# A spectral filter gated with a state-space scan: one addition moved from VectorE into an accumulating DMA, skip rows and table steps re-ordered

## The chip, the cores and the metric

The kernel runs on one core of one Trainium2 chip. The core has TensorE (PE, matrix products into PSUM), VectorE (DVE), ScalarE (ACT), GpSimd (POOL), SyncE (SP, which issues most of the DMAs) and 16 DMA engines. The metric is device time in microseconds, the median of several executions.

## The reference

Two branches read the same `x` (2048 positions by 1024 channels, bf16) and are mixed by a gate per position:

```python
g = sigmoid((x * gate_w).sum(-1, keepdims=True))
# branch A: a filter in the two-dimensional spectrum
X = rfft2(x, axes=(-2, -1)) * (w_r + 1j * w_i)
a = irfft2(X, s=(S, D), axes=(-2, -1)).astype(bfloat16)
# branch B: a diagonal complex state-space model, 1024 states
Lam = Lambda_re + 1j * Lambda_im;  dt = exp(log_dt)
Lam_bar = exp(dt * Lam)
B_bar = ((Lam_bar - 1.0) / Lam)[:, None] * (B_re + 1j * B_im)
Bu = einsum("bld,pd->blp", x, B_bar)
for t in range(L): h = Lam_bar[None, :] * h + Bu[:, t, :]
b = 2.0 * einsum("blp,dp->bld", hseq, C_re + 1j * C_im).real + x * Dskip
return g * a + (1 - g) * b
```

## The kernel before, in words

**Branch A (FFT).** Both transforms are products with constant matrices. `fstage` adds and subtracts the input rows and multiplies by `FW_sb` (first stage). The main loop `fft_main` then runs over 16 groups of row frequencies. For group g, `fd(g)` does the column transform into PSUM (`ps_d`) and ACT copies it to `X1`; `bf_w(g)` does the row transform (`ps_xe`, `ps_xo`), copies it to `X` and multiplies by the weights `W` on VectorE (`Y`, L525 to L528); `bi(g)` transforms the rows back (`ps_q`). The order is fd(g+2), bf_w(g+1), bi(g). A second loop over 8 pairs (`idm`, `pm`, `fi`) does the inverse column transform and writes branch A to a scratch in DRAM, `ya_scratch`. These PSUM tiles share a pool of three buffers.

**Branch B (scan).** Time is cut into NCH = 4 chunks c of TC = 512 positions, and the 1024 states into 4 groups q of 256: 16 tiles (c, q). The complex recurrence is turned by an angle that grows with time, so that what is left is a real scan with a real factor. For each tile:

- `ssm_pe` (L388) multiplies `xT` by `BT`: 32 matmuls of 128x512 in 4 blocks of 8, one PSUM tile `psu` each (two buffers); ACT evicts and scales each block into the tile `u` (L390, two buffers).
- `ssm_dve` turns `u` forward (two products L399 and L401, one addition L403, into `cu`), scans four times (L408, into `su`), keeps the last column as the carry (L417 to L421) and turns back: two products L433 and L435 with the table reversed in time, and an addition L437 into `h`. As written, L435 puts the second product into `u` itself, and L437 adds `cu` and `u`. Where `h` lies (`h_tile`): chunks 0 and 3 in a pool of four buffers, chunk 1 in free parts of `big`, chunk 2 in parts of `xT`. `cu` and `su` have two buffers each.

The sines and cosines of the angle are in `tab`; `tables(q)` makes them when chunk 0 comes to tile q. For q < 2 VectorE computes the angle, for q of 2 and 3 ACT does (L360); VectorE takes the fraction of a turn in three steps over both halves at once (`frac`, L288 to L290, 1024 fp32 elements per partition), ACT applies Sin twice (L366, L367), VectorE negates one (L368).

**Output.** For each block tb of 128 positions, `half(tb, dh)` (L782) does 16 matmuls of `h` with `CT[dh]` for each half dh of the channels, into `psy` (three buffers). After the second half VectorE computes `o` = `psy` * (1-g) + `xf` (L789), and SP writes `o` out. `xf` is made ahead of that: SP loads rows of `x` (`xc`) and of branch A (`gac`); `prep_d` multiplies `xc` by `Dskip` on VectorE (L760); `prep_a` scales both on ACT (L764, L766) and GpSimd issues a DMA that adds `gac` into `xf` (L767). `prep_a(tb)` also issues the loads of block tb+2.

**What sets the order.** The kernel is written as two generators, the FFT (`fft_main`) and the scan (`ssm_all`), which are stepped in turn by estimated clocks `fft.t` and `ssm.t`: a line of constants near L725 says how far the scan may be for each state of the FFT, another (L728) up to where it is run before the output starts, and later L805 and L812 interleave the scan with the output blocks (`c_all`). In `ssm_all` the VectorE part of a tile runs one tile behind its matmuls; every step of `ssm_dve` ends in a `yield`. SP and GpSimd keep the written order throughout, ACT from the output part on; the order of the others is made by a scheduler that starts from this order and its own estimates. Every engine then works its list strictly in that order. `pre` in `c_all` says after which half block each `prep_d` and `prep_a` is written.

Of the kernel before, what the change touches and what calls it, by code (L numbers as in the profile page):

```python
# [10 lines left out]
ACT = mybir.ActivationFunctionType  # L11
ALU = mybir.AluOpType
FP32 = mybir.dt.float32
BF16 = mybir.dt.bfloat16
I32 = mybir.dt.int32
# [7 lines left out]
P = 128  # L23
TC = 512
NCH = S // TC
MAGIC = 12582912.0
# [110 lines left out]
def kernel(  # L137
# [17 lines left out]
    nc = tc.nc  # L155
# [130 lines left out]
    def frac(xx, n, nm, pool=sp, tag=None):  # L286
        kk = pool.tile([P, n], FP32, name=nm + "_k", **({"tag": tag} if tag else {}))
        nc.vector.tensor_scalar(out=kk, in0=xx, scalar1=MAGIC, scalar2=-MAGIC, op0=ALU.add, op1=ALU.add)  # L288
        nc.vector.tensor_sub(out=xx, in0=xx, in1=kk)
        nc.vector.tensor_scalar(out=kk.bitcast(I32), in0=xx.bitcast(I32), scalar1=0x7FFFFFFF, scalar2=None,  # L290
                                op0=ALU.bitwise_and)
        return xx, kk
# [57 lines left out]

    def tables(q):
        xa = rp.tile([P, 2 * TC], FP32, name="xa", tag="cu")
        for jj in range(2):
            jb = 2 * q + jj
            xj = xa[:, TC * jj:TC * (jj + 1)]
            if q < 2:
                nc.vector.tensor_scalar(out=xj, in0=tau_f, scalar1=thp[:, jb:jb + 1], scalar2=beta[:, jb:jb + 1],
                                        op0=ALU.mult, op1=ALU.add)
            else:
                nc.scalar.activation(out=xj, in_=tau_f, func=ACT.Identity, scale=thp[:, jb:jb + 1],  # L360
                                     bias=beta[:, jb:jb + 1])
        rr, ra = frac(xa, 2 * TC, "xa", rp, "su")
        tq = tab[:, 2 * q:2 * q + 2]
        rr = rr.rearrange("p (a t) -> p a t", a=2)
        ra = ra.rearrange("p (a t) -> p a t", a=2)
        nc.scalar.activation(out=tq[:, :, 0, :], in_=ra, func=ACT.Sin, scale=-TWO_PI_LO, bias=chpi)  # L366
        nc.scalar.activation(out=tq[:, :, 1, :], in_=rr, func=ACT.Sin, scale=-TWO_PI_LO)  # L367
        nc.vector.tensor_scalar_mul(out=tq[:, :, 2, :], in0=tq[:, :, 1, :], scalar1=-1.0)  # L368


    hs = {}
# [22 lines left out]
    def ssm_dve(c, q, u):  # L394
        tq = tab[:, 2 * q:2 * q + 2]
        full = [P, 2, 2, TC]
        cu = rp.tile(full, BF16, name="cu", tag="cu")
        su = rp.tile(full, BF16, name="su", tag="su")
        nc.vector.tensor_mul(out=cu, in0=u, in1=tq[:, :, 0:1, :].to_broadcast(full))  # L399
        yield  # L400
        nc.vector.tensor_mul(out=su, in0=u[:, :, ::-1, :], in1=tq[:, :, 1:3, :])  # L401
        yield
        nc.vector.tensor_add(out=cu, in0=cu, in1=su)  # L403
        yield
        for jj in range(2):
            jb = 2 * q + jj
            for ri in range(2):
                nc.vector.tensor_tensor_scan(out=su[:, jj, ri, :], data0=r_sb[:, jb:jb + 1].to_broadcast([P, TC]),  # L408
                                             data1=cu[:, jj, ri, :],
                                             initial=(0.0 if c == 0 else carry[q][:, jj, ri:ri + 1]),  # L410
                                             op0=ALU.mult, op1=ALU.add)
                if not (jj and ri):
                    yield
        if c + 1 < NCH:
            ge = su[:, :, :, TC - 1]
            k1 = sm.tile([P, 2, 2], FP32, name="k1")
            nc.vector.tensor_mul(out=k1, in0=ge, in1=cTC[:, 2 * q:2 * q + 2].unsqueeze(2).to_broadcast([P, 2, 2]))  # L417
            k2 = sm.tile([P, 2, 2], FP32, name="k2")
            nc.vector.tensor_mul(out=k2, in0=ge[:, :, ::-1], in1=sg[:, 2 * q:2 * q + 2, :])
            cy = sm.tile([P, 2, 2], FP32, name=f"carry{q}")  # L420
            nc.vector.tensor_add(out=cy, in0=k1, in1=k2)  # L421
            carry[q] = cy
        yield
        h = h_tile(c, q)
        hs[c, q] = h
        if False:
            nc.vector.tensor_mul(out=h, in0=su, in1=tq[:, :, 0:1, ::-1].to_broadcast(full))
            yield
            nc.vector.tensor_mul(out=cu, in0=su[:, :, ::-1, :], in1=tq[:, :, 1:3, ::-1])
            nc.gpsimd.dma_start(out=h, in_=cu, accum_op=ALU.add)  # L430
            yield
            return
        nc.vector.tensor_mul(out=cu, in0=su, in1=tq[:, :, 0:1, ::-1].to_broadcast(full))  # L433
        yield
        nc.vector.tensor_mul(out=u, in0=su[:, :, ::-1, :], in1=tq[:, :, 1:3, ::-1])  # L435
        yield
        nc.vector.tensor_add(out=h, in0=cu, in1=u)  # L437
        yield
# [250 lines left out]
    def ssm_all():  # L689
        prev = iter(())  # L690
        for c in range(NCH):
            for q in range(4):
                if c == 0:
                    tables(q)
                u = up.tile([P, 2, 2, TC], BF16, name="u", tag="u")
                for i, _ in enumerate(ssm_pe(c, q, u)):
                    yield 0.5
                    for _ in range((0,4,3,3)[i]):
                        next(prev, None)
                        yield 0.52  # L700
                prev = ssm_dve(c, q, u)
        for _ in prev:
            yield 0.72
# [18 lines left out]
    ssm = Gen(ssm_all())  # L722
    fft = Gen(fft_main())
    while not fft.done:
        if ssm.t < (18.5 * (fft.t - 3.5) / (54.4 - 3.5) if fft.t < 54.4 else 18.5 + (44 - 18.5) * (fft.t - 54.4) / 35.0):  # L725
            ssm.step()
        else:
            fft.step()  # L728
    while ssm.t < 44:
        ssm.step()  # L730
    fctx.close()

    with ExitStack() as bctx:
# [59 lines left out]
        def c_all():  # L793
            order = [(0, 0), (1, 0), (2, 0), (0, 1), (1, 1), (2, 1)] + [(tb, dh) for tb in range(3, 16) for dh in range(2)]
            pre = {(0, 0): [(prep_d, 0), (prep_d, 1)], (1, 0): [(prep_a, 0)], (2, 0): [(prep_a, 1)],
                   (0, 1): [(prep_d, 2)], (1, 1): [(prep_a, 2)], (2, 1): [(prep_d, 3)], (3, 0): [(prep_a, 3), (prep_d, 4)],
                   (3, 1): [(prep_a, 4)]}
            for n in range(5, 16):
                pre[n - 1, 0] = [(prep_d, n)]
                pre[n - 1, 1] = [(prep_a, n)]  # L800
            for tb, dh in order:
                half(tb, dh)
                for f, n in pre.get((tb, dh), ()):
                    f(n)
                yield 3.6  # L805

        while ssm.t < 48:
            ssm.step()
        cg = Gen(c_all())
        t0 = ssm.t  # L810
        while not cg.done:
            if not ssm.done and ssm.t - t0 <= cg.t * 1.05:  # L812
                ssm.step()
            else:
                cg.step()
# [30 lines left out]
```

## Time and profile before

| | |
|---|---|
| median of 3 runs | 351.5 us (351.18 to 352.78) |
| the profiled execution's own time | 353.56 us |
| its span, first to last instruction | 351.8 us |
| granted TensorE clock | 0.99 |
| PE busy | 325.6 us, 93% of the span |
| DVE busy | 297.6 us, 85% |
| ACT busy | 188.0 us, 53% |
| POOL busy | 41.9 us, 12% |
| L437, last addition of the back rotation, 16 times | 1.22 us each |
| `xf` DMA with addition, 512 KB, 16 times | 4.0 us from issue to landing |

"Busy" is the time in which an engine has an instruction running. Matmuls are pipelined, so that the time of one (379 ns for 128x512) is longer than the distance between two starts (216 ns): the distance is what counts. The profile also answers what an engine waited for, which chain of work ended last, and what ran when; line numbers are those of the kernel before.

### The profile page before, as it was taken

Reading aid. Unit: us, or ns where it says so; the run is one execution under the profiler, and the core shown is the slowest. Engines: PE = TensorE matmul, PEld = TensorE weight load, DVE = VectorE, ACT = ScalarE, POOL = GpSimd, SP = SyncE. Lnnn points to the kernel's source line nnn. Section 1 sums busy time; section 2 is a strip of 40 time slices with the busy share of each in tenths; the row PEclk is TensorE's granted clock in tenths of the full one; section 3 lists DMA queues with packets and bytes.
Section 4 is the critical chain, followed back from the end, with each engine's and each line's share of the span. In section 5 each row is a group of like instructions: output and inputs, shape, how many; then the busy total and the mean of one; then the engine's idle time right before and its main releaser. Section 6 shows DMA issues by size and latency. Waiting matters only on the chain.

```text
span 351.8 us, 4890 instructions
## 1 busy us (share of the span) xinstructions
PE 325.6 (93%) x1804; PEld 173.6 (49%) x1804; DVE 297.6 (85%) x419; ACT 188.0 (53%) x255; POOL 41.9 (12%) x89
## 2 busy tenths in 40 slices
PE   3788999889979999999999999999989998999995
PEld 1565565556545656564444444444434443444442
DVE  4998848986999969898999999989898898988431
ACT  1987969759948887587344314432413404322330
POOL 5330412112210000000011000000000000000110
PEclk9999999989989999999999999999999999999999
DMA  7979999969997022113897053422414223444963
GB/s 263 352 104 224 215 238 198 185 152 194 196 227 134 33 89 89 61 60 121 229 223 204 3 179 67 143 89 60 136 36 129 91 60 104 108 134 136 265 197 106
DMA packets 68168, 51.30 MB, mean 146 GB/s; under 512 B 52656, under 2 KB 55728, under 8 KB 68144
## 3 DMA queue, kind: packets, MB, share of 16 engines
q1 hardware_dynamic: 64144, 38.75, 43.6%
q0 software_dynamic: 3648, 12.07, 13.6%
q8 instruction: 14, 0.23, 0.3%
q10 hardware_dynamic: 352, 0.17, 0.2%
q14 instruction: 10, 0.08, 0.1%
HBM read 21.61 MB, written 8.39 MB: 85 GB/s over the span
## 4 chain that ended last, share of the span: by engine, by line
PE 63%; DVE 18%; DMA 7%; ACT 5%; issue 3%; SPq 1%; POOL 0%; DVEq 0%; ACTq 0%; POOLq 0%
PE psy L782 27%; PE psu L388 22%; DVE su L408 6%; DMA xt<-in_A_x_dram 3%; PE ps_id L557 3%; PE ps_d L488 2%; DMA xc<-in_A_x_dram 2%; DMA MM<-c_MM 1%; DVE cu L403 1%; DMA xT<-in_A_x_dram 1%; DVE cu L433 1%; DVE t L526 1%; PE ps_q L546 1%; PE ps_y L576 1%; PE ps_q L547 1%
## 5 line engine op out<-in xcount | busy, mean ns | idle before, releaser
L388 PE MATMUL psu<-xT,BT 128*128 128x512 bf16 x512 | 120.3, 379 | 4.5 <-ACT u L390 3.1
L388 PEld LDWEIGHTS <-BT 128*128 128x128 bf16 x512 | 49.7, 98 | 60.1 <-issue 5.9
L408 DVE TENSOR_TENSOR_SCAN su<-r_sb,carry,cu 128x512 bf16<-128x512 f32 x48 | 57.7, 1264 | 0.4
L390 ACT ACTIVATE u<-psu,rho 128x512 bf16<-128x512 f32 x32 | 22.1, 691 | 64.5 <-PE psu L388 46.7
L782 PEld LDWEIGHTS <-h 128*128 128x128 bf16 x256 | 25.1, 98 | 30.2
L767 POOL DMA_DIRECT2D xf<-gac x16 | 14.0, 875 | 215.4 <-ACT xf L766 201.5
L390 ACT ACTIVATE u<-psu,nrho 128x512 bf16<-128x512 f32 x32 | 22.1, 691 | 29.3 <-PE psu L388 29.3
L764 ACT ACTIVATE gac<-gac,gf 128x1024 bf16<-128x1024 bf16 x16 | 18.3, 1141 | 27.8 <-DMA gac<-ya_scratch 27.8
L782 PE MATMUL psy<-big,h 128*128 128x512 bf16 x128 | 28.9, 379 | 0.0
L782 PE MATMUL psy<-CT,h 128*128 128x512 bf16 x128 | 28.9, 379 | 0.0
L789 DVE SCALAR_TENSOR_TENSOR o<-psy,om_f,xf 128x1024 bf16<-128x1024 f32 (+1 forms) x17 | 20.6, 1214 | 7.0 <-PE psy L782 7.0
L760 DVE TENSOR_TENSOR xc<-xc,dsk_bc 128x1024 bf16<-128x1024 bf16 x16 | 11.0, 686 | 17.1 <-DMA xc<-in_A_x_dram 17.1
L399 DVE TENSOR_TENSOR cu<-u,tab 128x2048 bf16<-128x2048 bf16 x16 | 19.5, 1219 | 5.0 <-ACT u L390 4.8
L550 ACT CAST big<-ps_q 128x1024 bf16<-128x1024 f32 x16 | 16.4, 1026 | 11.2 <-PE ps_q L549 11.0
L546 PE MATMUL ps_q<-MM,Y 128*128 128x256 bf16 x64 | 16.3, 287 | 4.7 <-DVE Y L527 4.5
L782 PEld LDWEIGHTS <-big 128*128 128x128 bf16 x128 | 12.5, 98 | 15.1
L782 PEld LDWEIGHTS <-xT 128*128 128x128 bf16 x128 | 12.5, 98 | 15.1
L403 DVE TENSOR_TENSOR cu<-cu,su 128x2048 bf16<-128x2048 bf16 x16 | 19.6, 1226 | 0.3
L433 DVE TENSOR_TENSOR cu<-su,tab 128x2048 bf16<-128x2048 bf16 x16 | 19.5, 1219 | 0.1
L488 PE MATMUL ps_d<-G_sb,big 128*128 128x256 bf16 (+3 forms) x128 | 19.6, 294 | 0.0
L401 DVE TENSOR_TENSOR su<-u,tab 128x2048 bf16<-128x2048 bf16 x16 | 19.5, 1218 | 0.0
L435 DVE TENSOR_TENSOR u<-su,tab 128x2048 bf16<-128x2048 bf16 x16 | 19.5, 1217 | 0.0
(168 smaller groups left out, 559.6 us busy)
## 6 DMA issues: line engine op xcount, KB each, us to landing
xf<-gac POOLq DMA_DIRECT2D x16, 512.0 KB, 4.0
ya_scratch<-ya SPq DMA_DIRECT2D x16, 256.0 KB, 2.0
xc<-in_A_x_dram SPq DMA_DIRECT2D x16, 256.0 KB, 2.9
gac<-ya_scratch SPq DMA_DIRECT2D x16, 256.0 KB, 3.1
out_dram<-o SPq DMA_DIRECT2D x15, 256.0 KB, 2.0
MM<-c_MM SPq DMA_DIRECT2D x16, 192.0 KB, 4.3
xt<-in_A_x_dram SPq DMA_DIRECT2D x4, 512.0 KB, 4.3
CT<-in_A_x_dram SPq DMA_DIRECT2D x4, 512.0 KB, 7.8
```

The lines of the kernel that those rows point to most:

```text
L388: nc.tensor.matmul(psu, lhsT=BT[:, jb, ri, dblk, :], rhs=xT[:, dblk, TC * c:TC * (c + 1)], start=(dblk == 0), stop=(dblk == 7))
L390: nc.scalar.activation(out=u[:, jj, ri, :], in_=psu, func=ACT.Copy, scale=(nrho if ri else rho)[:, jb:jb + 1])
L399: nc.vector.tensor_mul(out=cu, in0=u, in1=tq[:, :, 0:1, :].to_broadcast(full))
L401: nc.vector.tensor_mul(out=su, in0=u[:, :, ::-1, :], in1=tq[:, :, 1:3, :])
L403: nc.vector.tensor_add(out=cu, in0=cu, in1=su)
L408: nc.vector.tensor_tensor_scan(out=su[:, jj, ri, :], data0=r_sb[:, jb:jb + 1].to_broadcast([P, TC]), data1=cu[:, jj, ri, :], initial=(0.0 ...
L433: nc.vector.tensor_mul(out=cu, in0=su, in1=tq[:, :, 0:1, ::-1].to_broadcast(full))
L435: nc.vector.tensor_mul(out=u, in0=su[:, :, ::-1, :], in1=tq[:, :, 1:3, ::-1])
L488: nc.tensor.matmul(ps[:, lo:lo + w], lhsT=FX[:, q, 8 * g:8 * g + 8, :], rhs=G_sb[:, o:o + w], start=start, stop=stop, skip_group_check=True)
L546: nc.tensor.matmul(dst, lhsT=Yr[:, e:e + 255:2], rhs=ri_, start=True, stop=False, **kw)
L782: nc.tensor.matmul(psy[:, ds], lhsT=hs[c, jb // 2][:, jb % 2, ri, P * tq:P * (tq + 1)], rhs=CT[dh][:, jb, ri, :], start=(i == 0), stop=(i ...
L789: nc.vector.scalar_tensor_tensor(out=o[:, ds], in0=psy[:, ds], scalar=om_f[:, tb:tb + 1], in1=xfs[tb][:, ds], op0=ALU.mult, op1=ALU.add)
```

## The change

- `ssm_dve`: for chunks 2 and 3, except tile (3, 3), the first back product goes straight into `h`, the second into `cu`, and the addition is a DMA issued by GpSimd that adds `cu` into `h`. `u` is then no longer written by the second product. The other nine tiles are as before.
- `tables`: each half (512 elements) is handled by itself with steps of its own, which the scan's generator issues one at a time.
- the pacing constants: 18.5 becomes 17, 44 becomes 42, 48 becomes 47, 1.05 becomes 1.08.
- `pre`: `prep_d(n)` is written behind the second half of block n-2 instead of the first half of block n-1, and the pair is issued from one list, `prep_a` first.

```diff
     def tables(q):
         xa = rp.tile([P, 2 * TC], FP32, name="xa", tag="cu")
+        kk = rp.tile([P, 2 * TC], FP32, name="xa_k", tag="su")
+        tq = tab[:, 2 * q:2 * q + 2]
         for jj in range(2):
             jb = 2 * q + jj
-            xj = xa[:, TC * jj:TC * (jj + 1)]
+            xj, kj = xa[:, TC * jj:TC * (jj + 1)], kk[:, TC * jj:TC * (jj + 1)]
             if q < 2:
                 nc.vector.tensor_scalar(out=xj, in0=tau_f, scalar1=thp[:, jb:jb + 1], scalar2=beta[:, jb:jb + 1],
                                         op0=ALU.mult, op1=ALU.add)
+                yield
             else:
                 nc.scalar.activation(out=xj, in_=tau_f, func=ACT.Identity, scale=thp[:, jb:jb + 1],
                                      bias=beta[:, jb:jb + 1])
-        rr, ra = frac(xa, 2 * TC, "xa", rp, "su")
-        tq = tab[:, 2 * q:2 * q + 2]
-        rr = rr.rearrange("p (a t) -> p a t", a=2)
-        ra = ra.rearrange("p (a t) -> p a t", a=2)
-        nc.scalar.activation(out=tq[:, :, 0, :], in_=ra, func=ACT.Sin, scale=-TWO_PI_LO, bias=chpi)
-        nc.scalar.activation(out=tq[:, :, 1, :], in_=rr, func=ACT.Sin, scale=-TWO_PI_LO)
+            nc.vector.tensor_scalar(out=kj, in0=xj, scalar1=MAGIC, scalar2=-MAGIC, op0=ALU.add, op1=ALU.add)
+            yield
+            nc.vector.tensor_sub(out=xj, in0=xj, in1=kj)
+            nc.vector.tensor_scalar(out=kj.bitcast(I32), in0=xj.bitcast(I32), scalar1=0x7FFFFFFF, scalar2=None,
+                                    op0=ALU.bitwise_and)
+            yield
+            nc.scalar.activation(out=tq[:, jj, 0, :], in_=kj, func=ACT.Sin, scale=-TWO_PI_LO, bias=chpi)
+            nc.scalar.activation(out=tq[:, jj, 1, :], in_=xj, func=ACT.Sin, scale=-TWO_PI_LO)
         nc.vector.tensor_scalar_mul(out=tq[:, :, 2, :], in0=tq[:, :, 1, :], scalar1=-1.0)
+        yield
...
-        if False:
+        if (c>=2 and (c,q)!=(3,3)):
             nc.vector.tensor_mul(out=h, in0=su, in1=tq[:, :, 0:1, ::-1].to_broadcast(full))
             yield
             nc.vector.tensor_mul(out=cu, in0=su[:, :, ::-1, :], in1=tq[:, :, 1:3, ::-1])
             nc.gpsimd.dma_start(out=h, in_=cu, accum_op=ALU.add)
             yield
             return
...
                 if c == 0:
-                    tables(q)
+                    for _ in tables(q):
+                        yield 0.0
...
-        if ssm.t < (18.5 * (fft.t - 3.5) / (54.4 - 3.5) if fft.t < 54.4 else 18.5 + (44 - 18.5) * (fft.t - 54.4) / 35.0):
+        if ssm.t < (17 * (fft.t - 3.5) / (54.4 - 3.5) if fft.t < 54.4 else 17 + (42 - 17) * (fft.t - 54.4) / 35.0):
...
-    while ssm.t < 44:
+    while ssm.t < 42:
...
-                   (0, 1): [(prep_d, 2)], (1, 1): [(prep_a, 2)], (2, 1): [(prep_d, 3)], (3, 0): [(prep_a, 3), (prep_d, 4)],
-                   (3, 1): [(prep_a, 4)]}
-            for n in range(5, 16):
-                pre[n - 1, 0] = [(prep_d, n)]
-                pre[n - 1, 1] = [(prep_a, n)]
+                   (0, 1): [(prep_d, 2)], (1, 1): [(prep_a, 2), (prep_d, 3)], (2, 1): [(prep_a, 3), (prep_d, 4)]}
+            for n in range(4, 16):
+                pre.setdefault((n - 1, 1), []).append((prep_a, n))
+                if n < 15:
+                    pre.setdefault((n - 1, 1), []).append((prep_d, n + 1))
...
-        while ssm.t < 48:
+        while ssm.t < 47:
...
-            if not ssm.done and ssm.t - t0 <= cg.t * 1.05:
+            if not ssm.done and ssm.t - t0 <= cg.t * 1.08:
```

## Prediction

> **What bounds it now.** I read the page's busy shares first, then its slices, then the waits of each engine in the last part, then the chain there and the order of time around each hole of TensorE.
>
> ```profile
> PE 325.6 (93%) x1804; PEld 173.6 (49%) x1804; DVE 297.6 (85%) x419; ACT 188.0 (53%) x255; POOL 41.9 (12%) x89
> ...
> PE   3788999889979999999999999999989998999995
> ...
> PEclk9999999989989999999999999999999999999999
> ```
>
> TensorE is the bound: sixteen 128x512 matmuls take 3.45 us in the chain, 0.216 each, so the 512 of L388 and the 512 of L782 are 221 us and the FFT's about 90. That is 311 of a span of 351.8; only the other 41 can be won. Some 15 lie before 30 us (loading) and 4 behind the last matmul, both untouched. What the edits can reach are holes of TensorE: those of the spectral loop (30 to 112 us, some 15 us of loss) and those of the last part (164 to 348 us). The waits of TensorE and of ScalarE, from 160 us on:
>
> ```profile
> PE psu L388 <- ACT u L390: 3.1, 3, 1.4
> ...
> ACT u L390 <- DVE xT L437: 11.0, 2, 6.4
> ACT u L390 <- DVE h L437: 6.8, 1, 6.8
> ```
>
> So in the last part TensorE loses 3.1 us, three times: `psu` is not evicted because `u` is not free, and `u` is not free because VectorE still reads it in the last addition (L437) of two tiles before. VectorE's round there, as the chain between 255 and 300 us gives it:
>
> ```profile
> 261.22 1.29 DVE o L789
> ...
> 262.95 2.72 DMA xc<-in_A_x_dram
> ...
> 265.69 0.69 DVE xc L760
> 266.39 1.15 DVE cu L403
> ...
> 267.56 4.82 DVE su L408 x4
> ...
> 272.40 1.22 DVE cu L433
> 273.63 1.15 DVE u L435
> ```
>
> A tile starts at 262.4 and the next at 277.1: VectorE needs 14.7 to 15.6 us for a tile of chunks 2 and 3, with 0.9 to 1.6 us of waiting for `xc`; TensorE needs 13.8 for its share (32 matmuls of each kind). The holes of the loop, in order of time, VectorE's row and then TensorE's, twice:
>
> ```profile
> 63.52 3.45 DVE L408 TENSOR_TENSOR_SCAN su<-r_sb,cu 128x512 bf16<-128x512 f32 x3
> 71.64 0.28 PE L546 MATMUL ps_q<-MM,Y 128*128 128x256 bf16 x1 [2.29 <-DVE Y L527]
> 94.24 3.45 DVE L408 TENSOR_TENSOR_SCAN su<-r_sb,cu 128x512 bf16<-128x512 f32 x3
> 102.37 0.28 PE L546 MATMUL ps_q<-MM,Y 128*128 128x256 bf16 x1 [2.26 <-DVE Y L527]
> ```
>
> Three scans, a table step and a product stand in a row on VectorE, the frequency rows' `Y` waits behind them, and TensorE for `Y`. After each hole the 256-wide matmuls start every 0.21 us instead of 0.11 for some 3.6 us: each costs about 3.8 us, not 2.3.
>
> **What the Trainium skill says.** "TensorE: Matmul & The Clock Gate", Part 1, What's actually happening: an idle TensorE falls to half its clock and needs about 3.4 us of work to get it back. The trace agrees (0.21 against 0.11, 3.6 us), though waits of about 2.3 us were enough here, while one of 1.6 us at 43 us was not. "DMA: Bandwidth & Descriptors", Rules for kernel authors: an accumulating DMA reads its destination and writes it later, so readers of `h` must wait for its landing. "SBUF — State Buffer", Who interferes with whom: a product of two tensors has no mode that takes GpSimd's write port, so VectorE's products should not starve the descriptors. Of the 16 `xf` DMAs, issued amid such work, the issue took 0.86 to 0.95 us.
>
> **The change, part by part.**
>
> *The addition.* Seven tiles (all of chunks 2 and 3 but the last) lose L437: 7 x 1.14 us (start to start; 1.22 alone) = 8.0 us off VectorE. The first product now goes into `h`, the second into `cu`, so nothing after L401 touches `u`: it comes free about 10 us sooner. With that the three TensorE waits go: 0.95 + 0.75 + 1.39 = **-3.1 us**. VectorE's round falls to 13.0 plus about 1 of `xc`, level with TensorE's 13.8, and the lead of the evictions (5 to 8 us in the trace) absorbs the rest. The other 5 us of the 8.0 are worth nothing: TensorE hides them. For them to matter the last tile's `h` (done at 321.9, wanted by the thirteenth matmul of block 12 at 322.5) would have to be late; in the new order it has some 5 us.
>
> Added are seven DMAs of 512 KB on GpSimd's queue. No row shows this one; nearest is
>
> ```profile
> xf<-gac POOLq DMA_DIRECT2D x16, 512.0 KB, 4.0
> ```
>
> The skill's fit ("DMA: Bandwidth & Descriptors", Anatomy of one DMA: 2.0 us plus bytes over 436 KB per us) gives an estimate of 3.2; I take 4 to 5, and 8 as upper end (twice `xf`, since the source is twice as large and chunk 2's destination lies in four pieces per partition). Issue: 0.9 us, at most four times that. Who waits: `cu` is wanted again two tiles on, about 13 us after the product, and block 8 or 12 of L782 later still. Up to 12 us it costs nothing; beyond that VectorE stops. The queue is in order: the new order has xf 0 to 3, tile (2,0), xf 4, (2,1), (2,2), xf 5, (2,3), then one xf and one tile by turns. So xf 5 now waits for the product of (2,2): about 241 against 238.4, landing by 247 where its reader stood at 261. Nothing on the path.
>
> *Skip rows.* In the order of VectorE and ACT `xc` and `gac` still follow the output of three blocks before; each pair of ACT copies stands one eviction later in most tiles. Row 3's product moves ahead of tile (1,3): perhaps 1 us of VectorE's wait, away from the path. Zero; from -0.3 to +0.5.
>
> *Table steps.* Per table two halves instead of one piece: three fp32 steps of 0.68, 1.216 and 0.69 become pairs of about 0.37, 0.63 and 0.37 (half the elements plus some 0.05 each): +0.15 us, four tables +0.6 on VectorE. The Sins, 1.17 and 1.07 at 1024, become two each of about 0.65: +0.35, four tables +1.4 on ACT. Counts: VectorE +12 - 7, ACT +8.
>
> *The order that results.* The pacing constants (17 for 18.5, 42 for 44, 47 for 48) move 5 L388 matmuls (1.1 us) behind the sixteenth frequency group and 8 (1.7 us) from the inverse stage to the last part: they are only put off, TensorE has the same total. What counts is holes. I walked the new order from group 5 with the durations above (a full product 1.13 and a scan 1.14 start to start, `Y` of a group 1.2 for its two products and 0.67 for its sums, each ACT copy 0.7 or 1.0). First tile: `Y` of 6 ends at 64.25; scan 65.4; `Y` of 7 with a scan in it 68.4; scan 69.55; table 2's subtraction 70.15. Its Sin now stands on ACT ahead of X1(9): 70.85, X1(9) 71.9. Group 7's `ps_q` needs the PSUM buffer that X1(9) empties, and TensorE has been out of work since 69.5: it starts at 71.9, against 71.6 before. **The first hole stays** (0 +- 1). From there to group 12 ACT paces both. Second tile: `Y` of 11 ends at 87.9; two products, a table step and an addition 91.6; `Y` of 12 with a scan 94.6; 13 waits for its X until 95.1 and ends, with a scan, at 98.1. TensorE comes to `ps_q` of 13 at 99.0 instead of 102.4, without a hole. Then two scans, a subtraction, the carry's small steps and a product: 102.3; `Y` of 14 with a product in it is half done at 105.0, where TensorE had run dry at 102.8: a new hole of 2.2. `Y` of 15, with the addition in it, lets `ps_q` start at 108.3 against 110.45: -2.1, less the 1.1 put off: **-1.0**. If the clock falls after the new hole, 1.2 comes back. At the inverse stage about 1.6 us of table 3 is still owed on VectorE, and four stages of `ps_y` on I find -0.7 left. I take **-0.6** for all before 164 us; bounds -4.5 (neither hole, no half clock) to +5 (a third one).
>
> Sum: -3.1 - 0.6 = -3.7: span 351.8 to 348.1. The profiled run itself took 353.6, its span 351.8, and the median of the three is 351.5; taking the difference over, **347.8 us**.
>
> **Rivals.**
> *More than that* (17%): both holes shrink below what lets the clock fall. For it: the longest row of VectorE work between two `Y` falls from 5.2 to 4.5 us. Against: ACT, busy 4 to 5 us of every 5 in most of the loop, gets more work, and so paces what VectorE lets go. Half of the two holes' 7.6 is then won, -3.8, and -3.1 from the last part: about 344.6.
> *The loop gives back what the last part wins* (19%): a half-clock spell at groups 7 and 14 both, with one more behind the first inverse `pm`: +1.5 to +3.5 on -3.1, about 350.5 to 352, no change to be told.
> *Slower* (14%): ACT's queue. Sins wait there for single VectorE steps, and X1, the PSUM buffers and so TensorE wait behind them. One such place costs 2.4 us and 1.5 of half clock, 3.9. There are four Sins each for tables 2 and 3; it decides once two more of them bind than I found: +7.8 - 3.1, about 355. Against: those of table 3 come when their inputs are done, by my walk.
> *The DMA is late* (within the slower case, 3%): landing beyond 12 us would stop `cu`; the `xf` rows (3.9 to 7.1) speak against.
> *Nothing changes in the last part*: `u` free sooner, but evictions held by something else. ACT's pair for block k wants `xc` of k, prepared about 15 us before it; so no (in the 19%).
>
> **How the numbers follow.** Main case 50% (346 to 349.7), with 17% below it: faster by over 0.5% (which is about what a measurement here can tell from no change, 1.8 us) 0.67; same 0.19; slower 0.14. The range leaves out half the slower case and the far end of the good one: 344.3 to 352.5. The likeliest alone: 346 to 349.7.
>
> **What would show it.** `psu` waits of TensorE after 160 us near 0 and no wait of ACT's `u` for L437's successor in chunks 2 and 3; accumulating DMAs landing in 4 to 8 us; VectorE's tile at 13.5 to 14 us; TensorE waits for `ps_q` at groups 7 and 14 of 2 to 2.5 us, none near group 13; the end of the inverse stage near 162. Wrong if the loop's `ps_q` waits sum to over 7 us, if X1 stands behind Sins more than once, or if `cu` waits for a DMA.

## The result, and the profile after

The changed kernel takes 371.7 us (median of four runs, 368.0 to 373.4) where the kernel before, run beside it, takes 352.1: a ratio of 1.052 [1.041, 1.063] (of the means; the numbers in brackets are a 95% interval). Some executions fall into a slower state with a lower clock; ratios leave them out, and as E8's profiled execution was one of them, its profile isn't used below. The changed kernel is slower by 5%, on the far side of every case that the prediction named. The profiled execution took 368.0 us with a span of 366.2, which is 14.4 more than before.

The page of the changed kernel: busy times, then the slices for TensorE, VectorE and the clock.

```profile
PE 324.1 (89%) x1773; PEld 173.1 (47%) x1804; DVE 289.3 (79%) x424; ACT 189.5 (52%) x263; POOL 49.9 (14%) x96
...
PE   3888799798988998989999999999999899059995
...
DVE  4999559978999687969999994949587694997242
...
PEclk9999999999999999999999999999999999759999
```

VectorE has 8.3 us less to do, as foreseen, and TensorE has the same work. But TensorE has a slice of 0 at 312 to 320 us (a slice is 9.2 us) and half a slice after it, with the clock down to 0.5 to 0.7 in the same place. From 220 us on every second slice or so of VectorE is a four or a five, where it showed eights and nines before (the row of the kernel before):

```profile
DVE  4998848986999969898999999989898898988431
```

VectorE has less work and is idle more. The waits after 160 us, of the changed kernel, name what VectorE waits for:

```profile
ACT gac L771 <- DMA gac<-ya_scratch: 48.0, 8, 17.2
DVE xc L767 <- DMA xc<-in_A_x_dram: 38.4, 10, 5.3
...
PE psy L789 <- DVE o L796: 13.5, 1, 13.5
ACT u L396 <- DVE su L407: 12.8, 3, 7.2
...
PE psu L394 <- ACT u L396: 1.8, 1, 1.8
```

Of the kernel before, the same wait of VectorE:

```profile
DVE xc L760 <- DMA xc<-in_A_x_dram: 17.1, 9, 3.5
```

(Each line gives us in total, number of waits, longest.) In the seven tiles `ACT u` no longer waits for the addition but for L407, which is the early release of `u` that the prediction counted on, and TensorE's three `psu` waits of 3.1 us have become one of 1.8. In their place stands one wait of 13.5 us: TensorE has done all its `psu` and `psy` that it may, the three buffers of `psy` are full, and VectorE's output `o` of block 8 is late. VectorE is late because it waited for `xc`, a row of `x` that the skip product reads: 38.4 us in all (17.1 before), of which 26 fall ahead of that wait of TensorE (7 before). The DMA issues of the changed kernel (line, engine, count, KB each, median us from issue to landing):

```profile
xf<-gac POOLq DMA_DIRECT2D x16, 512.0 KB, 5.5
...
xc<-in_A_x_dram SPq DMA_DIRECT2D x16, 256.0 KB, 4.8
gac<-ya_scratch SPq DMA_DIRECT2D x16, 256.0 KB, 4.7
```

Before, `xf` stood at 4.0 us, and the two loads at

```profile
xc<-in_A_x_dram SPq DMA_DIRECT2D x16, 256.0 KB, 2.9
gac<-ya_scratch SPq DMA_DIRECT2D x16, 256.0 KB, 3.1
```

One block shows how that comes about. ScalarE's copy for `xf`, then GpSimd's, SyncE's and VectorE's rows between 236 and 262 us of the changed kernel, each in order of time (start, duration, instruction, and in brackets the idle time before it and what ended it):

```profile
236.91 1.14 ACT L773 ACTIVATE xf<-xc,om_f 128x1024 f32<-128x1024 bf16 x1
```

```profile
253.25 1.26 POOL L436 DMA_DIRECT2D xT<-cu  x1 [16.29 <-DVE cu L435]
254.01 1.41 POOL L774 DMA_DIRECT2D xf<-gac  x1
```

```profile
253.91 0.34 SPq L798 DMA_DIRECT2D out_dram<-o  x1
254.34 0.38 SPq L750 DMA_DIRECT2D xc<-in_A_x_dram  x1
254.81 0.41 SPq L754 DMA_DIRECT2D gac<-ya_scratch  x1
```

```profile
251.46 1.22 DVE L435 TENSOR_TENSOR cu<-su,tab 128x2048 bf16<-128x2048 bf16 x1
252.60 1.28 DVE L796 SCALAR_TENSOR_TENSOR o<-psy,om_f,xf 128x1024 bf16<-128x1024 f32 x1
253.79 1.22 DVE L405 TENSOR_TENSOR cu<-u,tab 128x2048 bf16<-128x2048 bf16 x1
254.93 1.22 DVE L407 TENSOR_TENSOR su<-u,tab 128x2048 bf16<-128x2048 bf16 x1
260.17 0.69 DVE L767 TENSOR_TENSOR xc<-xc,dsk_bc 128x1024 bf16<-128x1024 bf16 x1 [4.03 <-DMA xc<-in_A_x_dram]
```

Within 1.6 us five transfers are issued: 512 KB into `h` (here a part of `xT`), 512 KB into `xf`, and 256 KB each of output, `xc` and `gac`, 1792 KB in all. The `xf` one, of block 5, had its data ready at 238.05, when ScalarE's copy ended (copy and transfer are each the sixth of their kind in the trace); it stood 16 us in GpSimd's queue behind the DMA into `h`, which waited for the product in `cu`. So both are let go together, and at the very moment in which `o`, the next instruction on VectorE, lets go of SyncE's three. The `xc` load needs 5.8 us, and the third instruction behind `o` reads it. VectorE's tiles (from L405 to the next L405) take 16.1 to 17.3 us from 219 us on, where TensorE's share takes 13.8; after some six of them the backlog stops TensorE.

Before, the same multiply stood just as close behind its load (262.95 and 265.69 in the rows shown of the chain), but with one transfer fewer, and with `xf` following 4 us later. Its wait was 0.9 us there:

```profile
265.69 0.69 DVE L760 TENSOR_TENSOR xc<-xc,dsk_bc 128x1024 bf16<-128x1024 bf16 x1 [0.93 <-DMA xc<-in_A_x_dram]
```

### The profile page after: what moved, and what is told of

It reads as the page before. It is cut to its first block, busy times and chain, and to the rows that moved or that the text cites. A ratio compares the mean times of both kernels' runs of the same rounds, so it can differ in the third digit from the quotient of the medians.

```text
span 366.2 us, 4894 instructions
## 1 busy us (share of the span) xinstructions
PE 324.1 (89%) x1773; PEld 173.1 (47%) x1804; DVE 289.3 (79%) x424; ACT 189.5 (52%) x263; POOL 49.9 (14%) x96
## 4 chain that ended last, share of the span: by engine, by line
PE 39%; DVE 36%; DMA 14%; issue 5%; ACT 3%; SPq 2%; POOL 0%; DVEq 0%; ACTq 0%; POOLq 0%
PE psy L789 19%; PE psu L394 14%; DVE su L414 11%; DMA xc<-in_A_x_dram 8%; DVE cu L409 3%; DVE cu L405 2%; DVE o L796 2%; DVE su L407 2%; DVE t L532 2%; DVE cu L435 2%; DMA MM<-c_MM 2%; PE ps_d L494 2%; DMA CT<-in_A_x_dram 1%; DVE Y L531 1%; DMA xT<-in_A_x_dram 1%
## 5 line engine op out<-in xcount | busy, mean ns | idle before, releaser
L394 PE MATMUL psu<-xT,BT 128*128 128x512 bf16 x492 | 116.6, 379 | 5.4 <-ACT u L396 1.8
L767 DVE TENSOR_TENSOR xc<-xc,dsk_bc 128x1024 bf16<-128x1024 bf16 x16 | 10.9, 689 | 38.4 <-DMA xc<-in_A_x_dram 38.4
L774 POOL DMA_DIRECT2D xf<-gac x16 | 15.8, 1025 | 131.4 <-PE psu L394 75.6
L789 PE MATMUL psy<-CT,xT 128*128 128x512 bf16 x63 | 16.8, 425 | 13.6 <-DVE o L796 13.5
L405 DVE TENSOR_TENSOR cu<-u,tab 128x2048 bf16<-128x2048 bf16 x16 | 19.5, 1219 | 7.8 <-ACT u L396 7.8
L407 DVE TENSOR_TENSOR su<-u,tab 128x2048 bf16<-128x2048 bf16 x16 | 19.5, 1218 | 0.0
L552 PE MATMUL ps_q<-MM,Y 128*128 128x256 bf16 x64 | 15.1, 273 | 4.7 <-ACT X L506 2.5
L414 DVE TENSOR_TENSOR_SCAN su<-r_sb,cu 128x512 bf16<-128x512 f32 x16 | 19.0, 1211 | 0.0
L494 PE MATMUL ps_d<-G_sb,big 128*128 128x256 bf16 (+3 forms) x128 | 18.8, 286 | 0.1
```

The costliest lines, as they stand in the source:

```text
L394: nc.tensor.matmul(psu, lhsT=BT[:, jb, ri, dblk, :], rhs=xT[:, dblk, TC * c:TC * (c + 1)], start=(dblk == 0), stop=(dblk == 7))
L494: nc.tensor.matmul(ps[:, lo:lo + w], lhsT=FX[:, q, 8 * g:8 * g + 8, :], rhs=G_sb[:, o:o + w], start=start, stop=stop, skip_group_check=True)
L774: nc.gpsimd.dma_start(out=xf, in_=gac, accum_op=ALU.add)
L789: nc.tensor.matmul(psy[:, ds], lhsT=hs[c, jb // 2][:, jb % 2, ri, P * tq:P * (tq + 1)], rhs=CT[dh][:, jb, ri, :], start=(i == 0), stop=(i ...
```

## The experiments

My theory after this reading: the bytes of the accumulating DMAs, let go together with `xf`, the output and the next loads, make the `xc` load late, and VectorE's queue stands at its multiply. Rivals: the skip rows that begin sooner do it alone; the table steps and the new pace do it; the DMA into `h` does it by its own latency or by its place in GpSimd's queue, whatever its size.

The kernel before ran between 350 and 360 us beside the experiments, above the 351.5 of the first three runs, so ratios are compared. Spans, waits and landings are those of one profiled execution each; executions of one kernel can lie 5 us apart (E1: 358.3 to 363.1), so a difference of a few us between two spans is not told from noise.

| kernel | span of the profiled run | ratio to before | `xc` waits | `xc` landing | TensorE waits for `o` |
|---|---|---|---|---|---|
| before | 351.8 | 1 | 17.1 | 2.9 | none |
| changed | 366.2 | 1.052 [1.041, 1.063] | 38.4 | 4.8 | 13.5 |
| E1, no DMA into `h` | 356.5 | 1.024 [1.012, 1.036] | 21.6 | 3.4 | none |
| E2, old skip rows | 362.8 | 1.035 [1.027, 1.043] | 35.2 | 4.1 | 10.9 |
| E3, tables and pace alone | 355.7 | 1.021 [1.008, 1.035] | 21.6 | 2.9 | none |
| E4, `xc` loaded a block ahead | 368.0 | 1.048 [1.039, 1.057] | 34.7 | 4.3 | 12.8 |
| E5, changed, written order | 349.1 | 1.0025 [0.9995, 1.0055] | 0.8 | 3.4 | none |
| E6, before, written order | 353.5 | 1.013 [1.007, 1.019] | 1.9 | 3.2 | none |
| E7, before, DMAs, written order | 345.8 | 0.988 [0.983, 0.992] | 0.7 | 3.5 | none |
| E8, E7 and sooner skip rows | – | 0.986 [0.983, 0.989] | – | – | – |
| E9, DMAs of 2 KB | 349.1 | 0.999 [0.996, 1.0025] | 23.0 | 3.7 | none |
| E10, E5 with the old pace | 348.8 | 0.9915 [0.989, 0.994] | 0.7 | 3.1 | none |
| E11, E5 with the old tables | 351.0 | 1.002 [0.998, 1.005] | 1.0 | 3.5 | none |
| E12, before, DMAs alone | 363.4 | 1.034 [1.029, 1.039] | 41.0 | 4.7 | 14.0 |

Waits are sums over the profiled execution, landings medians, in us.

### E1 to E3: one part undone, and both

E1, the DMA undone in the changed kernel:

```diff
-        if (c>=2 and (c,q)!=(3,3)):
+        if False:
```

> The changed kernel with the seven accumulating DMAs into h taken back (the sum is VectorE's again), everything else kept. Theory (three transfers at once: the accumulating DMA into h, the one into xf, which the earlier skip rows moved to the same moment, and the loads of xc and gac; the xc load lands late and VectorE's queue stands at its multiply): two of the three remain, the xc load lands in 3.5 to 4.5 us, VectorE waits 1.5 to 2.5 us a block for it, 353 to 358 us. Rival 'the earlier skip rows alone do it': still 367 to 373 us, xc waits near 38 us in all. Rival 'table steps and pace do it': 367 to 373 us with the loss before 164 us. Rival 'the DMA into h by itself, late for TensorE': about 351 us and xc landing as before the change, 2.9 us.

E2, the positions of the skip rows undone (the list `pre` as before):

```diff
-            pre = {..., (1, 1): [(prep_a, 2), (prep_d, 3)], (2, 1): [(prep_a, 3), (prep_d, 4)]}
+            pre = {..., (1, 1): [(prep_a, 2)], (2, 1): [(prep_d, 3)], (3, 0): [(prep_a, 3), (prep_d, 4)], (3, 1): [(prep_a, 4)]}
...
```

> The changed kernel with the skip rows put back half a tile later; accumulating DMAs and table steps kept. Theory (three transfers at once): the xf transfer falls 13 us after the loads again, two of three remain, xc lands in 4 to 5 us, VectorE waits 2 to 3 us a block, 354 to 360 us. Rival 'skip rows alone': 347 to 352 us. Rival 'table steps and pace': 367 to 373. Rival 'the DMA into h by itself': 367 to 373 us, whatever xc does.

E3 has both edits, so that table steps and pace are left.

> The changed kernel with both the accumulating DMAs and the earlier skip rows taken back: only the table steps and the new pace are left. Theory, and every rival but one: 350 to 353 us, xc landing 2.9 us, xc waits about 17 us in all. Rival 'table steps and pace do it': 367 to 373 us.

The four corners by span are 355.7 (neither), 356.5 (skip rows), 362.8 (DMAs) and 366.2 (both): the DMAs cost 7.1 us alone and 9.7 with the sooner skip rows, the skip rows 0.8 alone and 3.4 with the DMAs. By the ratios the DMAs cost 1.4% and 2.8%, the skip rows 0.3% and 1.7%, with intervals of about 1% to either side of each ratio, so that of these only the 2.8% is well clear of the noise, with the 1.7% at its edge. Neither rival that blames one of the other parts alone stands: the skip rows alone add next to nothing, and table steps and pace alone come to 1.021, not 1.052.

E1 came out above the 353 to 358 us of the theory (360.3), E2 above its 354 to 360 (364.6). For E1, E3 gives a reason: table steps and pace, which I had put at nothing, cost some 2% here, with an interval of 1.3% to either side. That was a miss of the theory too, and E10 and E11 return to it. It doesn't explain E2: the same DMAs and skip rows without table steps and pace (E12) are at 1.034, level with E2's 1.035. What the parts cost doesn't simply add up in the planner's order.

E2 helped so little because with the old skip rows, too, `xf` is issued in the same moment. ScalarE's and GpSimd's rows of E2, block 5:

```profile
237.20 1.13 ACT L773 ACTIVATE xf<-xc,om_f 128x1024 f32<-128x1024 bf16 x1
```

```profile
248.85 1.26 POOL L436 DMA_DIRECT2D xT<-cu  x1 [16.27 <-DVE cu L435]
249.61 1.41 POOL L774 DMA_DIRECT2D xf<-gac  x1
```

The copy is done at 238.3, and its transfer waits 11.3 us until the one that needs `cu` has gone. Here it is the queue that sets the time, not the moment at which ScalarE has its copies ready.

### E4: loading `xc` a block sooner, which did nothing

```diff
-            xcs[tb] = fin.tile([P, D], BF16, name="xc", bufs=2)
+            xcs[tb] = fin.tile([P, D], BF16, name="xc", bufs=3)
...
+        load_xc(2)
...
+            if tb + 3 < 16:
+                load_xc(tb + 3)
             if tb + 2 < 16:
-                load_xc(tb + 2)
...
-    tau_f = cpool.tile([P, TC], FP16, name="tau_f")
+    tau_f = tab[:, 7, 2, :].bitcast(FP16)
```

> The changed kernel with everything kept, but xc in three buffers instead of two and each load of xc issued one block earlier (the small table of positions moves into a dead slot to make room). The same transfers still run together; the loads only have a whole block more before VectorE reads them. Theory: the xc waits fall from 38 to under 3 us, VectorE's tile from 16.7 to 13.2 to 14 us, TensorE's wait of 13.5 us for o goes, 346 to 351 us, though the landing times stay at 4 to 6 us. Rival 'the DMA into h by itself is late for TensorE or holds cu': 360 us or more. Rival 'the transfers slow VectorE's own instructions in SBUF': 360 or more with longer VectorE instructions.

It took 368.0 by span and waited 34.7 us for `xc`, where the theory had expected under 3. The time is what the two rivals gave (360 us or more), but not for their reasons: no engine waits for `h` or `cu` in the trace, and VectorE's products last 1.22 us here as in the kernel before. SyncE's queue and VectorE's of this kernel, one block:

```profile
240.31 0.38 SPq L750 DMA_DIRECT2D xc<-in_A_x_dram  x1
```

```profile
240.90 1.22 DVE L407 TENSOR_TENSOR su<-u,tab 128x2048 bf16<-128x2048 bf16 x1
246.64 0.69 DVE L768 TENSOR_TENSOR xc<-xc,dsk_bc 128x1024 bf16<-128x1024 bf16 x1 [4.52 <-DMA xc<-in_A_x_dram]
```

The load stands a block sooner in the program, and the multiply still sits right behind it. VectorE's order is not the written one in this part: a planner places its instructions (in this part only ScalarE and SyncE are bound to the program's order; GpSimd, other than the section on the kernel before says, is bound only ahead of it), and it pulls the multiply forward, apparently to where it thinks that the load has landed. Given an earlier load it pulled by a whole block. So the wait is made in two steps: VectorE comes to the multiply 1.8 us behind the issue of its load, and in the crowd the load takes 5.3 to 6.4.

### E5 to E8, E12: the order of VectorE held still

```diff
-        bctx.enter_context(tc.manual_schedule(engines=set(getattr(mybir.EngineType, e) for e in ('Activation','SP'))))
+        bctx.enter_context(tc.manual_schedule(engines=set(getattr(mybir.EngineType, e) for e in ('Activation','SP','DVE'))))
```

E5 is the changed kernel with this line.

> The changed kernel, every transfer kept, but in the last part VectorE takes its instructions in the order in which the code writes them, as ScalarE and SyncE already do; the planner no longer pulls the multiply of xc forward to right behind the load that was issued a microsecond earlier. In the written order the multiply reads a row that was loaded a whole block before. Theory (the planner's pull exposes VectorE to the landing of the load, and the crowd of transfers makes that landing 5 to 6 us): xc waits fall from 38 to under 5 us in all, landings stay at 4 to 6 us, TensorE's 13.5 us wait for o goes, 348 to 356 us. Rival 'the accumulating DMA itself comes too late, or it slows VectorE in SBUF': 365 us or more. Rival 'the written order puts o behind waits of its own': o waits for psy or xf of 10 us or more in all, 360 or more.

E6 is the kernel before with this line alone.

> The kernel before, with VectorE's instructions of the last part in written order and nothing else. Theory: the 17 us of xc waits fall under 4, VectorE's tile from 14.7 to 13.9 us, so that TensorE's 3 us of psu waits shrink; 347 to 351.5 us, a ratio of 0.985 to 1.0. Rival 'xc waits of before were free': ratio 1.0 within 0.005. Rival 'the written order is worse for o': ratio above 1.01.

E7 adds to E6 the condition of the accumulating DMAs, E8 to that the changed kernel's list `pre`.

```diff
-        if False:
+        if (c>=2 and (c,q)!=(3,3)):
```

> The kernel before with the seven accumulating DMAs and the written order on VectorE in the last part; old skip rows, old table steps, old pace. Theory: crowding no longer reaches VectorE, its tile is 13 us, under TensorE's 13.8; psu waits near 0 after 160 us; 345 to 350 us. Rival 'the DMA into h costs by itself': 353 or more, TensorE waiting for h or VectorE for cu.

> As the one before, and the skip rows half a tile sooner too: the whole change but for the table steps and the pace, VectorE in written order. Theory: within 1 us of the run without the sooner skip rows; against the changed kernel in written order it tells what table steps and pace cost in time: 2 to 4 us less than that one. Rival 'table steps and pace cost nothing, the 1.02 of their run alone was the chip': equal to it within 1 us.

E12 is the kernel before with this condition alone, in the planner's order.

> The kernel before with the accumulating DMAs alone, VectorE's order by the planner: fourth corner beside the kernel before, its written order (1.013) and its written order with the DMAs (0.988). Theory (the DMAs cost only where the planner puts the multiply of xc right behind its load): xc landing 4 to 5 us, xc waits over 28 us, 356 to 364 us, ratio 1.01 to 1.035. Rival 'with the old table steps and pace the DMAs pay in any order': ratio under 1.0.

With E12 the square of order and DMAs is complete, on the old tables and pace:

| | planner's order | written order |
|---|---|---|
| addition on VectorE | 1 | 1.013 |
| accumulating DMA | 1.034 | 0.988 |

The DMAs lose 3.4% in one order and win 2.5% in the other. E5's rows show what differs. VectorE and SyncE of the changed kernel in written order, one block:

```profile
267.82 1.26 DVE L796 SCALAR_TENSOR_TENSOR o<-psy,om_f,xf 128x1024 bf16<-128x1024 f32 x1
269.00 0.68 DVE L767 TENSOR_TENSOR xc<-xc,dsk_bc 128x1024 bf16<-128x1024 bf16 x1
```

```profile
255.46 0.51 SPq L750 DMA_DIRECT2D xc<-in_A_x_dram  x1
...
269.54 0.41 SPq L750 DMA_DIRECT2D xc<-in_A_x_dram  x1
```

The multiply at 269.00 has its row from the load at 255.46, a block before; the load at 269.54 is for the next one. The `xc` waits fall to 0.8 us. The expectation that landings stay at 4 to 6 us failed: `xc` landed in 3.4, since in this order `o` is taken between two scans, 6 us away from the product that releases the DMA into `h`, and the transfers spread out by themselves. So E5 takes away both the crowd and the exposure, and doesn't say which of them is worth more; E9 does that for the crowd.

E6 missed its expectation on the slow side, where its second rival had put it (above 1.01). Removing the `xc` waits in this way gave the kernel before nothing: in its trace ScalarE's evictions still wait for the addition that reads `u` (8.7 us before the one at 233.8 us, ended by L437), TensorE's `psu` waits rise to 5.4, and `o` waits once 5.7 us for `xf`. The DMAs cure just that: in E7 TensorE has no wait at all after 160 us, and VectorE's tile, shown here by its first product in two tiles running, takes 12.6 us:

```profile
258.30 1.22 DVE L399 TENSOR_TENSOR cu<-u,tab 128x2048 bf16<-128x2048 bf16 x1
...
264.32 1.26 DVE L789 SCALAR_TENSOR_TENSOR o<-psy,om_f,xf 128x1024 bf16<-128x1024 f32 x1
...
269.12 1.22 DVE L429 TENSOR_TENSOR cu<-su,tab 128x2048 bf16<-128x2048 bf16 x1
270.25 0.68 DVE L760 TENSOR_TENSOR xc<-xc,dsk_bc 128x1024 bf16<-128x1024 bf16 x1
270.86 1.22 DVE L399 TENSOR_TENSOR cu<-u,tab 128x2048 bf16<-128x2048 bf16 x1
```

E7 (348.1 us) and E8 (348.8 us, over more runs) beat the kernel before by 1.2 to 1.4%, little but clear of the intervals, and the changed one by more. The sooner skip rows make no difference to be told between them.

E12 shows that the DMAs need neither the sooner skip rows nor the new pace to do harm.

### E9: the same order, without the bytes

```diff
-            nc.gpsimd.dma_start(out=h, in_=cu, accum_op=ALU.add)
+            nc.gpsimd.dma_start(out=h[:, 0, 0, 0:8], in_=cu[:, 0, 0, 0:8], accum_op=ALU.add)
```

> The changed kernel in its own order of instructions, with each of the seven accumulating DMAs cut from 2048 to 8 elements a partition: 2 KB instead of 512 KB. It leaves most of the second products out of h. The additions on VectorE stay away, the queues and the order stay the same; only the bytes go. Theory (the bytes of three or four transfers at once make the xc load late): xc landing falls from 4.8 to 3.5 us or less, xc waits from 38 to 15 to 25 us, TensorE's wait for o from 13.5 to under 4, 353 to 359 us. Rival 'not the bytes, but the DMA's place in the queue or its issue on GpSimd': 364 us or more, xc waits over 32 us.

VectorE's order is that of the changed kernel, instruction by instruction, and the seven DMAs still stand in the same queue. Only 510 of their 512 KB are gone, and with them 5% of the time: 0.999 against 1.052. From E9, GpSimd, SyncE and VectorE at a place like the one shown of the changed kernel:

```profile
260.37 0.86 POOL L436 DMA_DIRECT2D xT<-cu  x1 [13.45 <-DVE cu L435]
260.91 1.21 POOL L774 DMA_DIRECT2D xf<-gac  x1
```

```profile
261.49 0.38 SPq L750 DMA_DIRECT2D xc<-in_A_x_dram  x1
```

```profile
260.95 1.21 DVE L405 TENSOR_TENSOR cu<-u,tab 128x2048 bf16<-128x2048 bf16 x1
262.08 1.22 DVE L407 TENSOR_TENSOR su<-u,tab 128x2048 bf16<-128x2048 bf16 x1
264.81 0.69 DVE L767 TENSOR_TENSOR xc<-xc,dsk_bc 128x1024 bf16<-128x1024 bf16 x1 [1.51 <-DMA xc<-in_A_x_dram]
```

The load takes 3.3 us instead of 5.8 and VectorE waits 1.5 instead of 4.0. (The median landing of `xc`, 3.7, stayed a little above the 3.5 expected: `xf` still goes with the loads.) Over the whole kernel the `xc` waits are 23.0 us against 38.4, and TensorE's wait for `o` is gone. In the changed kernel's last part TensorE lost 13.5 us by that wait, 1.8 by `psu`, and 2.4 in the sixteen matmuls behind the wait, which ran in large part at half clock (6.04 us against 3.62): 17.7 in all, where the two spans differ by 17.1. This settles the place of the loss: the bytes of the DMAs, in an order that exposes VectorE to a load beside them. No trace shows a wait for `h` or for a DMA's release of `cu`, and VectorE's products last 1.22 us with the bytes and without, so neither the DMA's own latency nor a slower VectorE has a part in it. Not tried is `xf` ahead of the DMA into `h` in GpSimd's queue, which would say how much of the loss hangs on the two going together.

### E10 and E11: pace or table steps

Both stand on E5, whose last part has no exposure. E10 puts back the pace, E11 the tables in one piece.

```diff
-        if ssm.t < (17 * (fft.t - 3.5) / (54.4 - 3.5) if fft.t < 54.4 else 17 + (42 - 17) * (fft.t - 54.4) / 35.0):
+        if ssm.t < (18.5 * (fft.t - 3.5) / (54.4 - 3.5) if fft.t < 54.4 else 18.5 + (44 - 18.5) * (fft.t - 54.4) / 35.0):
...
-    while ssm.t < 42:
+    while ssm.t < 44:
...
-        while ssm.t < 47:
+        while ssm.t < 48:
...
-            if not ssm.done and ssm.t - t0 <= cg.t * 1.08:
+            if not ssm.done and ssm.t - t0 <= cg.t * 1.05:
```

```diff
-                    for _ in tables(q):
-                        yield 0.0
+                    tables(q)
...
```

> The changed kernel in written order on VectorE (353.9 us, ratio 1.0025) with the pace put back (18.5, 44, 48, 1.05); table steps one by one are kept. If the new pace is what costs 5 us there: 347 to 350 us, ratio 0.985 to 0.992. If the table steps cost it: 352.5 to 355 us, ratio 0.998 to 1.006.

> The changed kernel in written order on VectorE with the old tables in one piece; the new pace (17, 42, 47, 1.08) is kept. If the new pace costs 5 us: 352.5 to 355 us, ratio 0.998 to 1.006, with TensorE idle at 140 to 160 us. If the table steps do: 347 to 350 us.

E10 is at 0.9915 and E11 at 1.002, E5 at 1.0025, E8 at 0.986. So the new pace costs 1.1%, near 4 us, with the new tables, and 1.6% with the old (E11 against E8); the table steps cost about 0.5% (E10 against E8, whose intervals touch), and nothing that can be told where the pace is new (E11 against E5). Slices of the loop and the inverse stage, TensorE alone: the columns are the stretch, its length, TensorE's busy time with the number of records, the clock, the DMA share and GB/s. E5 (new pace) first, then E10 (old pace):

```profile
40.00:80.00 40.00, 36.19 (x267) 1.00 1.04 201
80.00:120.00 40.00, 35.98 (x241) 1.00 0.81 165
120.00:140.00 20.00, 20.00 (x138) 1.00 0.21 79
140.00:165.00 25.00, 22.09 (x124) 1.00 0.23 90
```

```profile
40.00:80.00 40.00, 37.33 (x267) 0.96 1.00 192
80.00:120.00 40.00, 34.24 (x237) 1.00 0.87 165
120.00:140.00 20.00, 20.00 (x119) 1.00 0.21 79
140.00:165.00 25.00, 24.59 (x163) 1.00 0.19 75
```

With the new pace TensorE is out of work for 2.9 us between 140 and 165 us, with the old one for 0.4. E11 shows the same 22.10 as E5. In the new-pace runs it waits there for VectorE, 1.6 us for `pm` and 1.3 for a row of the gate (`lrow`), where the old pace has one wait of 0.4. A `psu` wait of 2.0 us in the last part, in E5 and in E11 but not in E10, would be most of the rest. In the loop E5 has the better clock (1.00 against 0.96 in the first stretch), which gives back less than these two take. Why VectorE is late at 140 us with the new pace I did not take further: that fewer L388 matmuls are left to fill in there is an inference.

## Why the prediction was wrong

*What held.* In the kernel before, L437's read of `u` held the evictions, as said, and with the DMAs `ACT u` waits for L407 instead. The step "three TensorE waits go, -3.1" is right once VectorE isn't held elsewhere: none is left in E7. "VectorE's round falls to 13.0" measured 12.6 in E7. The landing of the DMAs was within what I allowed (5.7 us for rows of 4 KB, 7.7 for chunk 2's four pieces, 8 as upper end), and so was their issue (0.84 and 1.28). No `cu` of the last part was made late by them.

*What failed first.* "Added are seven DMAs ... Up to 12 us it costs nothing." I asked who reads what these DMAs write, and who writes what they read. I didn't ask what else is in transit in those 5 to 8 us. The profile had the answer: `xc`, whose load was issued 1.8 us before VectorE's in-order queue reached its reader, with a wait of 0.9 to 1.6 us already there. I wrote that wait into VectorE's round ("13.0 plus about 1 of `xc`") and left it as it was, though it is the landing time of a load less 1.8 us of cover (2.7 and 0.9 in the block shown of before, 5.8 and 4.0 in that of the changed kernel), and so passes on every us by which the load is slowed. It went to 3.6 to 5.3 us a block. E9 prices the omission: 5% of the time, from the bytes alone.

*What failed with it.* The walk of GpSimd's queue was right on the order ("one xf and one tile by turns"), put xf 5 at "about 241 against 238.4", where it went at 254.0, and asked only whether `xf` would be late for its own reader. It isn't, but for 1.6 us in all. But the queue's head waits for a product, and what it held is then released with it: 1 MB on the engines instead of half. For the skip rows I wrote "Zero; from -0.3 to +0.5". Without the DMAs the runs show nothing else (0.8 us by span). With them, in the planner's order, it is 3.4 by span and 1.7% by the ratios, at the edge of the noise.

*The pace.* "I take -0.6 for all before 164 us; bounds -4.5 to +5". By its holes the walk was good: TensorE waits 1.90 us for ScalarE's X at group 7, where the walk left 2.4 behind X1, and the second hole is at group 14, 1.68 us where I had 2.2. In the changed kernel, `ps_q` of both groups:

```profile
70.78 0.27 PE L552 MATMUL ps_q<-MM,Y 128*128 128x256 bf16 x1 [1.90 <-ACT X L506]
...
102.88 0.28 PE L552 MATMUL ps_q<-MM,Y 128*128 128x256 bf16 x1 [1.68 <-DVE Y L533]
```

Neither brings the clock down, as the two of the kernel before did. But I followed "four stages of `ps_y`" and then stopped; the loss of 2.5 us is behind them, in the inverse stage (E5 against E10). From its first `ps_q` to its last `ps_y` the changed kernel takes 126.4 us where the kernel before took 127.1, but with eight L388 matmuls, 1.7 us, put off: about +1 in place of -0.6. That the stage ends at 162.7, as "near 162" said, is luck, since this execution came to its first `ps_q` 1.1 us sooner. All this lies within the bounds given for the time before 164 us; the whole edit with its table steps and what it costs after that is 1.6% (E5 against E8) of 351.5 us, about 5.8, where I had allowed up to 5.

*The rivals.* Of the slower case I named two mechanisms, ScalarE's queue and a DMA so late that `cu` stops, and ruled the second out by the `xf` rows. Those rows gave the landing of a transfer that was issued 4 us behind the loads. The mechanism that decided was a DMA that is itself in time and makes another one late. The slower case was also put too near: 3.9 us twice less 3.1 is 356 rather than 355, and even that is some 15 us short of the changed kernel. (Likewise +1.5 to +3.5 on -3.1 is 349.9 to 351.9, where the second rival has 350.5 to 352.)

Taken without the bytes (E9), the changed kernel is level with the one before, and without table steps and new pace and with VectorE's order held (E8) it reaches 0.986, which on 351.5 us is 346.6. That lies near the forecast of 347.8, but no more than near: the forecast had a gain from the pace in it, and no change of VectorE's order.

## What to carry to other kernels

A transfer that replaces an engine's instruction has to be priced by what else is in transit when it goes: list the transfers that the same event releases, and look for a load that an in-order engine reads a few us after its issue, because any wait shown there grows one for one. Where a planner orders that engine, an earlier load or another buffer need not help, since the reader is pulled forward with it; hold the order first, then move the work. Holding the order is no gain by itself: without the DMAs it cost 1.3% here. And walk the queue for what it lets go at once, not only for what it delays.

## What the runs showed of the hardware

An accumulating DMA of 512 KB from SBUF to SBUF landed in 4.5 us with rows of 4 KB and in 5.4 with pieces of 1 KB (E5, E7), in 5.7 and 7.7 amid the crowd (changed, E2, E4); cut to 2 KB it took 2.0 to 2.1. The estimate of 3.2 from the Trainium skill ("DMA: Bandwidth & Descriptors", Anatomy of one DMA) was too low even for the first, and the measurement decides. Its issue on GpSimd took 0.84 us with whole rows and 1.28 in pieces. The loads of 256 KB beside it (`xc`) take 5.3 to 7.1 us in the chain of the changed kernel, where those in the chain of the kernel before took 2.7 and 3.4. In one such stretch of the changed kernel the DMA engines' mean busy share, as the profile counts it, is over 1:

```profile
257.00:261.00 4.00, 3.95 (x20) 1.78 (x19) 0.83 (x2) 0.00 (x0) 0.00 (x0) 1.00 1.13 252
```

The columns of this answer, which lists all engines, are the stretch, then TensorE, weight loads, VectorE, ScalarE and GpSimd busy, the clock, the DMA share and GB/s: VectorE works 0.8 us of these 4, while the transfers drain.

TensorE kept its full clock over waits of 1.68 and 1.90 us here, and lost it after waits of 2.26 and 2.29 in the kernel before. Between the two the length of the wait alone doesn't decide: one of 2.01 us in E5 left sixteen matmuls at 3.61 us, and one of 2.03 in E11 brought the clock to 0.69 in the stretch from 76 to 80 us. After the 13.5 us wait sixteen matmuls took 6.04 us instead of 3.62.
